# A pre-norm attention and feed-forward block on one core: the warming matmuls read a constant of ones, and some of them become 128 columns wide

## Chip, core and metric

The kernel runs on one core of one Trainium2 chip. The metric is device time in microseconds (us), the median of three executions. Five engines work side by side and meet at semaphores: TensorE (PE, with its weight loads shown apart as PEld), VectorE (DVE), ScalarE (ACT), GpSimd (POOL) and SyncE (SP), which issues nearly all of the transfers.

## What is computed

The input x has 2048 rows of 640 numbers in bf16. The block is a layer norm, a linear attention with 32 heads of 20 columns, a residual, a second layer norm, and a gated feed-forward layer of width 1536 with its residual:

```python
qkv = layernorm(x) @ wqkv                      # 640 -> 3 * 640
pq, pk = q @ w_phi[h], k @ w_phi[h]            # per head, 20 x 20
phi(p) = concat(softmax(p), softmax(-p))       # 40 features
kv, z = phi(pk).T @ v, sum(phi(pk))
o = (phi(pq) @ kv) / (phi(pq) @ z + 1e-6)
h = x + o @ wo
out = h + (gelu(layernorm(h) @ w_gate) * (layernorm(h) @ w_up)) @ w_down
```

The warming matmuls are no part of this. They multiply a constant by itself into a PSUM tile, `wu`, that nothing reads.

## The kernel before

The 2048 rows are 16 tiles of 128 rows, in four groups of four tiles. The order of work is written out by hand for all engines (the schedule is manual), so each engine runs its instructions in the order in which the code issues them.

The beginning is what matters for the change:

- Line 171 and on: SP issues the loads in one queue, one after another. First come tiles of x and pieces of the value weights `Wv`, then from line 188 five transposing loads of the key weights into `WkT` (line 186), one for each block of 128 input columns.
- Lines 194 to 197: DVE clears `zero`, a tile of 128 x 512, and then sets the ones columns of eight value tiles `vS`.
- Lines 207 to 212: TensorE runs nine warming matmuls of 512 columns, each with its own weight load, on `zero`.
- `ln_0` (line 246) computes the statistics of tile 0 and the centred tile `xc` (line 250). `tr_c(0)` transposes it on TensorE in five matmuls of 128 columns (line 147), and ACT copies the result to `LN1T` (line 148). `tr_c(1)` does this for tile 1, with the copy on DVE.
- `warm(WA)`, between the transposes of tile 0 and the first value matmuls, issues two more warming matmuls of 512 columns.
- `v_part` (line 290) multiplies the transposed tile by parts of `Wv`, as these arrive.
- `fold` (line 228) multiplies `WkT` by a block-diagonal matrix made of `w_phi`; five column blocks, the last of which needs the last of the five transposing loads. Copies on DVE (line 239) and ACT (line 237) bring the result to `Wk2`, which the key matmuls (line 274) need.

After that come a loop over the 16 tiles (keys, values and their products; the folded query weights; `load_T` of `WqT`), the query matmuls (line 362), the attention outputs, and the feed-forward layer (lines 615 and 636), which takes most of the time.

The tile `zero` lies in a pool `fp` that is closed before the loop. The framework that the kernel is written in has a preamble: POOL fills four one-column constants (line 749 in the profile, the place where the program is built), one of them 1.0 in bf16, and the engines then meet at a barrier before the body begins.

Of the kernel before, what the change touches and what calls it, by code (L numbers as in the profile page):

```python
# [8 lines left out]
BF16 = mybir.dt.bfloat16  # L9
# [8 lines left out]
def kernel(  # L18
# [12 lines left out]
    nc = tc.nc  # L31
    P = 128
# [11 lines left out]

    H0 = [(P * c) // Dh for c in range(NC)]
    NH = [(P * c + P - 1) // Dh - H0[c] + 1 for c in range(NC)]
    NWARM = 9
    VP = (0, 2, 4, 6, 9, 11)
    KA, QA = (1,3), (0,1,2,3,4)
    FQ = (4, 5, 6, 7, 8)  # L50

    QG = ((0, 1), (2, 3), (4, 5), (6,), (7, 8), (9, 10), (11, 12), (13, 14), (15,), (16,), (17,), (18,), (19,))
    QT = (15, 15, 15, 15)
    WA = 2
    T3 = 4

    KVG = {5: (0, 1), 9: (2, 3, 4, 5), 13: (6, 7, 8, 9), 15: (10, 11)}
# [42 lines left out]
    def gtile(name):  # L100
        return psG.tile([P, 2, 512], F32, name=name, tag="G")
# [62 lines left out]
    fp = fp_cm.__enter__()  # L164
# [26 lines left out]
    wu_v = B_w_up.rearrange("(c p) n -> p c n", p=P)  # L191


    zero = fp.tile([P, 512], BF16, name="zero")
    nc.vector.memset(zero, 0.0)
    for i in range(8):
        nc.vector.memset(vS[i][:, :, Dh], 1.0)
    make_identity(nc, ident)
# [6 lines left out]
                                compare_op=ALU.is_ge, fill=0.0, base=Dh - 1 - off, channel_multiplier=-1)  # L205

    wu = gtile("wu")
    def warm(n):
        for _ in range(n):
            nc.tensor.matmul(wu[:, 0, :], lhsT=zero[:, 0:P], rhs=zero, start=True, stop=True)  # L210

    warm(NWARM)

    def fold(WT, W2, halves, ds=range(NC)):

# [30 lines left out]
    def ln_0(t):  # L246
        xt, mean, rstd, _ = lnp[t] = ln_stats(p1, [x_sb[0][:, t, :]], f"c{t}", False, None, True)[0]
        nc.gpsimd.tensor_scalar(nrstd[t], rstd, -1.0, None, op0=ALU.mult)
        xc = fp.tile([P, D], BF16, name="xc", bufs=2)
        nc.vector.tensor_scalar(xc, xt, mean, None, op0=ALU.subtract)  # L250
        return xc

    def ln_st(*tiles, act=True, between=None, log=False):
        for t, v in zip(tiles, ln_stats(p1, [x_sb[t // 4][:, t % 4, :] for t in tiles], "1", act, between, log)):
            lnp[t] = v
# [138 lines left out]
    xc = [ln_0(t) for t in CT[:1]]  # L394
    tr_c(0)
    xc.append(ln_0(1))
    warm(WA)
    ln_st(2, act=False, log=True)
    v_part(0, 0, 1)
    tr_c(1)  # L400
# [364 lines left out]
```

## Time and profile before

| | |
|---|---|
| median of three executions | 279.65 us |
| the three executions | 279.73, 279.65, 278.71 us |
| profiled execution, first to last instruction (span) | 277.2 us |
| busy time of DVE, ACT, POOL | 167.3, 143.5, 94.7 us |
| warming matmuls | 11, the first at 1.24 us |
| first useful matmul (transpose of `xc`) | 4.73 us |
| DMA queues' share of 16 engines (first queue) | 30.8% |

The page gives no time of the profiled execution other than its span. The span is 2.45 us below the median and 1.5 us below the fastest of the three executions; start and end of an execution lie outside it.

How to read it: times in a timeline count from the first instruction of the span. A line of a timeline has the start, the length, the engine, the source line, the operation with what it writes and reads, and the count. In brackets stands the engine's idle time before it and what ended that idle time. A matmul's own time is its latency; several in a row overlap, so the distance from one start to the next is what one costs.

### The profile page before, as it was taken

Reading aid. Unit: us, or ns where it says so; the run is one execution under the profiler, and the core shown is the slowest. Engines: PE = TensorE matmul, PEld = TensorE weight load, DVE = VectorE, ACT = ScalarE, POOL = GpSimd, SP = SyncE. Lnnn points to the kernel's source line nnn. Section 1 sums busy time; section 2 is a strip of 40 time slices with the busy share of each in tenths; the row PEclk is TensorE's granted clock in tenths of the full one; section 3 lists DMA queues with packets and bytes.
Section 4 is the critical chain, followed back from the end, with each engine's and each line's share of the span. In section 5 each row is a group of like instructions: output and inputs, shape, how many; then the busy total and the mean of one; then the engine's idle time right before and its main releaser. Section 6 shows DMA issues by size and latency. Waiting matters only on the chain.

```text
span 277.2 us, 5817 instructions
## 1 busy us (share of the span) xinstructions
PE 271.6 (98%) x2337; PEld 172.1 (62%) x2337; DVE 167.3 (60%) x292; ACT 143.5 (52%) x239; POOL 94.7 (34%) x213
## 2 busy tenths in 40 slices
PE   7899999999999999999999999999999999999995
PEld 3677777764555887788754555675455567444574
DVE  6799999899496776675325757322666622233222
ACT  4879998778598755374524364413445440222200
POOL 4348997765202217365301353400226230000000
PEclk9999999999999999999999999999999999999999
DMA  7965732489730021324120213130022413000011
GB/s 204 192 232 112 99 74 47 44 256 393 255 102 0 4 47 36 85 49 77 30 65 2 47 27 63 32 88 33 14 36 25 73 25 95 26 0 0 0 50 47
DMA packets 42235, 21.37 MB, mean 77 GB/s; under 512 B 35040, under 2 KB 40416, under 8 KB 42208
## 3 DMA queue, kind: packets, MB, share of 16 engines
q1 hardware_dynamic: 42208, 21.01, 30.8%
q8 instruction: 18, 0.29, 0.5%
q14 instruction: 9, 0.07, 0.1%
HBM read 10.18 MB, written 2.62 MB: 46 GB/s over the span
## 4 chain that ended last, share of the span: by engine, by line
PE 87%; SPq 3%; DMA 3%; DVE 2%; ACT 2%; issue 1%
PE gu L615 38%; PE pd L636 19%; PE pq L362 8%; PE po L570 8%; PE pk L274 5%; PE pv L274 4%; PE ab L510 3%; PE kvp L340 2%; SPq L186 2%; DMA LN1T<-ln 2%; DVE stats L110 1%; DMA WkT<-in_A_wqkv_dram 1%; ACT E L307 1%; ACT ln L134 1%; PE wa L228 1%
## 5 line engine op out<-in xcount | busy, mean ns | idle before, releaser
L621 DVE TENSOR_TENSOR GT<-gu,g 128x512 bf16<-128x512 f32 (+1 forms) x60 | 34.4, 580 | 54.3 <-ACT g L618 54.1
L618 ACT ACTIVATE g<-gu 128x512 bf16<-128x512 f32 (+1 forms) x60 | 30.7, 512 | 69.3 <-PE gu L615 68.5
L615 PE MATMUL gu<-LN2T,Wg 128*128 128x512 bf16 (+1 forms) x300 | 61.9, 337 | 0.1
L615 PE MATMUL gu<-LN2T,Wu 128*128 128x512 bf16 (+1 forms) x300 | 61.8, 337 | 0.0
L636 PE MATMUL pd<-Wd,GT 128*128 128x320 bf16 (+2 forms) x396 | 53.8, 295 | 0.0
L636 PEld LDWEIGHTS <-GT 128*128 128x128 bf16 x396 | 37.9, 98 | 15.3 <-DVE GT L621 0.9
L615 PEld LDWEIGHTS <-Wu 128*128 128x128 bf16 x300 | 29.3, 98 | 22.6
L615 PEld LDWEIGHTS <-Wg 128*128 128x128 bf16 x300 | 28.3, 98 | 20.8
L274 PEld LDWEIGHTS <-LN1T 128*128 128x128 bf16 x290 | 27.9, 98 | 11.0 <-DMA LN1T<-ln 0.3
L322 POOL TENSOR_TENSOR vt<-vS,rs 128x672 bf16<-128x672 bf16 x22 | 29.1, 1344 | 9.1 <-DVE rs L318 7.4
L641 DVE TENSOR_TENSOR y<-pd,x_sb 128x640 bf16<-128x640 f32 (+3 forms) x18 | 13.5, 749 | 30.2 <-PE pd L636 30.2
L518 ACT COPY AB<-ab 128x704 f32<-128x704 f32 x28 | 19.6, 748 | 19.8 <-PE ab L510 19.6
L551 DVE TENSOR_TENSOR tt<-AB,w 128x1280 bf16<-128x1280 f32 x16 | 23.8, 1486 | 1.0 <-POOL w L544 0.9
L570 PE MATMUL po<-Wo,oT 128*128 128x320 bf16 x160 | 24.3, 299 | 0.0
L274 PE MATMUL pk<-Wk,LN1T 128*128 128x320 bf16 x160 | 24.0, 299 | 0.0
L314 DVE TENSOR_REDUCE sk<-E 128x64 f32<-128x1280 bf16 x16 | 22.9, 1434 | 1.2 <-ACT E L307 1.2
L362 PE MATMUL pq<-LN1T,Wq 128*128 128x512 bf16 x100 | 22.9, 379 | 0.0
L367 ACT ACTIVATE Eq<-pq 128x1024 bf16<-128x1024 f32 (+1 forms) x26 | 19.9, 830 | 2.4 <-PE pq L362 2.4
L307 ACT ACTIVATE E<-pk 128x640 bf16<-128x640 f32 x28 | 18.3, 716 | 4.5 <-PE pk L274 4.3
L570 PEld LDWEIGHTS <-oT 128*128 128x128 bf16 x160 | 15.6, 98 | 7.0 <-ACT oT L148 0.3
L274 PE MATMUL pv<-Wv,LN1T 128*128 128x320 bf16 x130 | 19.8, 299 | 0.2 <-DMA LN1T<-ln 0.2
L134 ACT ACTIVATE ln<-x_sb,v,rstd 128x640 bf16<-128x640 bf16 x14 | 12.9, 919 | 11.3 <-POOL v L598 11.1
(101 smaller groups left out, 268.1 us busy)
## 6 DMA issues: line engine op xcount, KB each, us to landing
out_dram<-y SPq DMA_DIRECT2D x15, 160.0 KB, 1.8
Wg<-in_B_w_gate_dram SPq DMA_DIRECT2D x1, 1920.0 KB, 9.4
Wu<-in_B_w_up_dram SPq DMA_DIRECT2D x1, 1920.0 KB, 15.3
Wd<-in_B_w_down_dram SPq DMA_DIRECT2D x1, 1920.0 KB, 7.9
x_sb<-in_A_x_dram SPq DMA_DIRECT2D x2, 640.0 KB, 5.5
Wo<-in_A_wo_dram SPq DMA_DIRECT2D x1, 800.0 KB, 11.1
x_sb<-in_A_x_dram SPq DMA_DIRECT2D x4, 160.0 KB, 3.1
Wv<-in_A_wqkv_dram SPq DMA_DIRECT2D x2, 320.0 KB, 4.1
```

Of the source, the lines that this page charges most:

```text
L274: nc.tensor.matmul(ps[:, u, 0:HD], lhsT=lnT(t, c), rhs=W[:, c, u * HD:(u + 1) * HD], start=(c == 0), stop=(c == NC - 1))
L307: nc.scalar.activation(Ek[t][:, s, :].rearrange("p (u f) -> p u f", u=2), pk[:, :, 0:HD], ACTF.Exp, scale=((lnp[t][2], nrstd[t]) if t in C ...
L314: nc.vector.reduce_sum(sk, Ek[t].rearrange("p s (h f) -> p (s h) f", f=Dh), axis=AX.X)
L322: eng.tensor_tensor(vt[:, s], vS[t % 8], rs[:, s * H:(s + 1) * H, None].to_broadcast([P, H, VC]), ALU.mult)
L362: nc.tensor.matmul(pqs[j][:, i, :], lhsT=Wq2[:, kc, c * P:(c + 1) * P], rhs=LN1T[b][:, kc, :], start=(kc == 0), stop=(kc == NC - 1))
L367: nc.scalar.activation(Eq[j][:, :, s, :], pqs[j][:, 0:len(QG[j])], ACTF.Exp, scale=(1.0, -1.0)[s])
L551: nc.vector.tensor_tensor(tt.rearrange("p s (h f) -> p s h f", f=Dh), num, w[:, :, :, None].to_broadcast([P, 2, H, Dh]), ALU.mult)
L570: nc.tensor.matmul(po[:, u, 0:HD], lhsT=st[t][:, c, :], rhs=Wo[:, c, u * HD:(u + 1) * HD], start=(c == 0), stop=(c == NC - 1))
L615: nc.tensor.matmul(gu[:, i, 0:n], lhsT=W[:, c, f * P:(f + 1) * P], rhs=LN2T[b][:, c, a0:a1], start=(c == 0), stop=(c == NC - 1))
L618: nc.scalar.activation(g[:, 0:n], gu[:, 0, 0:n], ACTF.Gelu_apprx_tanh)
L621: nc.vector.tensor_tensor(st[b, "g", f][:, a0:a1], gu[:, 1, 0:n], g[:, 0:n], ALU.mult)
L636: nc.tensor.matmul(pd[:, u, n0:n1], lhsT=st[b, "g", f][:, tl * P:(tl + 1) * P], rhs=Wd[:, f, u * HD + n0:u * HD + n1], start=(f == 0), sto ...
```

## The change

The tile `zero` and its clearing on DVE go. The warming matmuls read the preamble's constant of one bf16 column, seen as 128 x 512 by a column step of zero, for weights and for the moving operand alike. The function `warm` takes a list of widths. The nine matmuls of 512 columns at the start become seven of 512 and eight of 128 (4608 columns before and after); the two of 512 behind the transposes of tile 0 become seven of 128 (1024 columns before, 896 after). TensorE has 22 instructions more, DVE one fewer; the order of all others is the same on every engine.

```diff
-    NWARM = 9
...
-    WA = 2
...
-    zero = fp.tile([P, 512], BF16, name="zero")
-    nc.vector.memset(zero, 0.0)
+    ones = nc.const_aps.tensor(1.0, [P, 512], BF16)
     for i in range(8):
         nc.vector.memset(vS[i][:, :, Dh], 1.0)
...
     wu = gtile("wu")
-    def warm(n):
-        for _ in range(n):
-            nc.tensor.matmul(wu[:, 0, :], lhsT=zero[:, 0:P], rhs=zero, start=True, stop=True)
-
-    warm(NWARM)
+    def warm(*cols):
+        for n in cols:
+            nc.tensor.matmul(wu[:, 0, 0:n], lhsT=ones[:, 0:P], rhs=ones[:, 0:n], start=True, stop=True)
+
+    warm(*[512] * 7, *[P] * 8)
...
     xc = [ln_0(t) for t in CT[:1]]
     tr_c(0)
     xc.append(ln_0(1))
-    warm(WA)
+    warm(*[P] * 7)
     ln_st(2, act=False, log=True)
     v_part(0, 0, 1)
     tr_c(1)
```

## The prediction

> **What bounds the kernel now.** I read the page's busy times first, then the chain that ended last, then the timeline of TensorE over the first 16 us, where the change lies. The page says that the kernel as a whole is bound by TensorE:
>
> ```profile
> PE 271.6 (98%) x2337; PEld 172.1 (62%) x2337; DVE 167.3 (60%) x292; ACT 143.5 (52%) x239; POOL 94.7 (34%) x213
> ```
>
> 98% is an average, and the warming matmuls count as busy in it. What a change in the first 5 us is worth is read from the chain through the first 16 us. There, TensorE is not on it:
>
> ```profile
> 0.73 0.07 issue
> 0.79 0.40 SPq L171
> ...
> 5.20 1.30 SPq L186
> ...
> 9.18 1.28 SPq L186
> 10.46 0.04 issue
> 10.50 3.23 DMA WkT<-in_A_wqkv_dram
> 13.73 0.04 issue
> 13.77 0.51 PE wa L228 x6
> 14.28 0.02 issue
> 14.30 0.04 DVE Wk L239
> ```
>
> The columns are start, length and what it was. The reader is to see that from 0.79 to 10.5 us the chain is SP issuing one load after another: nine plain ones of 0.40 to 0.52 us and five transposing ones of about 1.28 us. It then waits 3.2 us for the last transposing load to land, and only at 13.77 us does it reach TensorE, with the fold that needs this load. No warming matmul, no transpose of `xc` and no value matmul is in it. After 14.3 us it goes on through DVE and ACT, whose busy shares from 16 to 28 us are nearly whole (DVE 3.90 of 4.00 and 7.93 of 8.00 us), and at 32.9 us it comes to TensorE to stay.
>
> The second view is the timeline of the first 6 us, TensorE's matmuls first, and then the last of its weight loads:
>
> ```profile
> 1.24 3.55 PE L210 MATMUL wu<-zero 128*128 128x512 bf16 x9 [1.24 <-DVE zero L195]
> 4.73 0.45 PE L147 MATMUL tp<-ident,xc 128*128 128x128 bf16 x5
> 5.02 0.59 PE L210 MATMUL wu<-zero 128*128 128x512 bf16 x2
> 5.96 0.72 PE L290 MATMUL pv<-Wv,LN1T 128*128 128x320 bf16 x4 [0.35 <-ACT LN1T L148]
> ```
>
> ```profile
> 3.35 0.15 PEld L210 LDWEIGHTS <-zero 128*128 128x128 bf16 x1 [0.27 <-issue]
> 3.78 0.15 PEld L210 LDWEIGHTS <-zero 128*128 128x128 bf16 x1 [0.28 <-issue]
> 4.20 0.10 PEld L210 LDWEIGHTS <-zero 128*128 128x128 bf16 x1 [0.27 <-issue]
> 4.72 0.28 PEld L147 LDWEIGHTS <-xc 128*128 128x128 bf16 x5 [0.43 <-DVE xc L250]
> ```
>
> Three things are to be seen. First, up to 4.20 us a warming matmul comes every 0.425 us, where a row of 10 matmuls of 512 columns in the feed-forward part takes 2.16 to 2.18 us on the chain, 0.217 each: TensorE runs at half its clock here, and the load at 4.20 us is the first short one (0.10 instead of 0.15 us). The granted clock in the profile reads 1.00 in these stretches too, so only the spacing shows the half clock. The clock rises about 2.95 us after the first warming matmul. Second, the transposes of tile 0 begin at 4.72 us since `xc` is done at 4.67 (it starts at 4.28 and takes 0.39), not since the warming matmuls end. Third, the value matmuls at 5.96 us wait for ACT's copy of the transposed tile (5.22 + 0.69 = 5.91), again not for the warming matmuls before them.
>
> **The change, part by part.**
>
> *The clearing of `zero` goes from DVE.* It is one instruction of 0.27 us at 0.91. DVE next sets eight columns of `vS` until about 2.3 us (1.25 + 1.08), and then idles 0.79 us until the first tile of x lands, at 3.12. So everything that DVE does for the chain starts when it does now: 0.
>
> *TensorE starts earlier.* Its first weight load waits for `zero` now (idle 1.24 us, released by DVE). The trace does not show when it would start without that wait. The earliest is 0.79 us, when SP, ACT and POOL leave the barrier; the latest is 1.24, as now. I take 0.91, where DVE, which waits at the same barrier, has its first instruction. That is 0.33 us earlier (bounds 0 and 0.45).
>
> *The first group has as many columns as before, 4608.* At 0.425 us per 512 columns this is 3.83 us, if the clock stays at half throughout. From 0.91 it ends at 4.74, against 5.07 now. If the clock rises at 4.18 us as in this execution, 3.27 us run at half clock (about 3940 columns), and the remaining 670 take 0.28 us at 0.217 per 512: the end is at 4.46. The eight narrow ones also need a weight load each. The five transposes show what that is at full clock: they last 0.45 us in all, 0.22 of it the latency of one, so (0.45 - 0.22) / 4 = 0.058 us each, against 0.054 for 128 columns at 0.217 per 512. That is nothing to speak of. In this execution, then, the group ends 0.2 us ahead of `xc`, and the transposes begin at 4.72 as before: 0.
>
> *The second group* is 7 x 0.058 = 0.41 us instead of 2 x 0.217 = 0.43, and ends near 5.45 us. The copy that the value matmuls wait for ends at 5.91: 0. Its cover is 0.46 us; at half clock the group would be 7 x 0.107 = 0.75 instead of 0.85.
>
> *The narrow width* matters where a useful matmul comes ready while a warming one runs. It then waits at most 0.107 us at half clock instead of 0.425. In this execution nothing waits so: 0. In one whose clock rises only after 4.7 us, the ninth wide matmul would end at 5.07 and hold the transposes back 0.35 us; with the change they would start at about 4.74. That is the place where the change can gain.
>
> *The reuse of memory and PSUM.* Without `zero` the pool is 1 KB per partition smaller, and a few waits of TensorE on its own and ACT's earlier work in PSUM differ: one is added at the transposes of the third tile, two of its own kind and two on ACT go. The added one asks for work of TensorE from some 2 us earlier, so it finds it done. I cost it at 0; at worst it drains one 320-column matmul, 0.299 - 0.136 = 0.16 us, and TensorE idles 0.79 us between 6 and 14 us, which covers it. The other four can only take waiting away, in the loop; the same 0.16 each bounds them, and DVE and ACT are late there: 0.
>
> **Weighing a rule.** The trace has the clock at half for the 2.95 us that follow the first matmul. [...]
>
> **The sum** on the profiled execution is 0: span 277.2 us stays. The time before, 279.65, is a median of executions that lie 1.0 us apart, with the profiled span 1.5 us below the fastest. If part of that spread is the moment at which the clock rises, an execution gains between 0 and the 0.33 us of the earlier start. I take the middle, 0.15: 279.5 us.
>
> **Rivals.**
>
> *Most executions have a late clock, and the path then goes through TensorE.* For it: two of three executions are 1.0 us above the third, and TensorE idles only 0.35 us before the first value matmuls and 0.79 us from there to 13.77, so that a clock at half to 7.6 us would use the slack up (work of about 1.5 us doubled, less 1.14, is +0.4). Against it: in the one trace the chain runs through SP. The gain would be the 0.33 us of the start, 0.16 us of half clock saved by an equally earlier rise, together 0.5, and at most the 1.0 us of the spread: 279.15, down to 278.7.
>
> *Slower: the constant read at column step zero streams slower than a dense tile.* No row before shows TensorE reading with step zero. It decides from the point at which the first group ends later than 4.72 plus the slack of 1.14, that is at 5.86 us: (5.86 - 0.91) / 4608 columns is 1.07 ns a column against 0.83 now, 30% slower. At twice the time the group would end at 0.91 + 7.66 = 8.57 us, the transposes would be 3.85 us late, less 1.14 of slack: +2.7, 282.3 us. The lower bound is the rate of now, 0.425 us per 512 columns, and I take it, as the nearest row is the same matmul at the same widths. [...]
>
> [...] A rise at 7.6 us instead of 4.2 costs the +0.4 worked out above: 280.05.
>
> *The change doesn't do what it says*: TensorE starts no earlier than 1.24 us, because something else holds it. Then everything is as now: 279.65. This falls together with the forecast.
>
> **Chances.** Forecast, hidden, 0.66 (its own range 278.7 to 280.0, from the spread of the three executions and the 0.33); late clock and a gain 0.18; clock later 0.10; slow reads 0.06. The range takes in the late clock's gain to a little below 278.7, since the median of three can fall on the fast executions, and the later clock above 280.05 by the same spread: 278.3 to 280.5. About 0.5%, 1.4 us, is what a measurement of this kernel can tell from no change. Faster by that (under 278.25) needs the late clock in nearly all executions and the full spread: 0.11. Slower by that (above 281.05) is the slow reads and a part of the later clock: 0.08. The rest, 0.81, is within.
>
> **What would show it.** In the profile after: the first warming matmul near 0.9 us with no wait on DVE; wide ones still 0.425 us apart before the rise of the clock and narrow ones at most 0.11; `xc`'s transposes still at about 4.7 us, released by DVE; value matmuls at about 5.96, released by ACT; and the last load of `WkT` landing at 13.7 with the fold waiting for it. I am wrong if the fold at 13.77 us or the key matmuls after it move by more than 0.3 us, if the wide warming matmuls are more than 0.5 us apart, or if the short weight loads begin later than 4.7 us.

## The result, and the profile after

The kernel after takes 281.24 us (median of six executions, 280.58 to 281.59), the kernel before 279.67 us (median of six, 278.71 to 279.91). The ratio is 1.0065, 95% interval 1.0044 to 1.0085: the medians lie 1.57 us apart and the means 1.79, on the slower side. Forecast were 279.5 us, in a range from 278.3 to 280.5. The profiled execution after took 281.43 us, and its span is 279.7 us, 2.5 more than before.

The first view is the timeline of TensorE over the first 6 us of the kernel after, in the columns used before:

```profile
0.83 4.00 PE L207 MATMUL wu<-const-bfloat16-1.0 128*128 128x512 bf16 x15 [0.83 <-PEq L746]
4.73 0.55 PE L145 MATMUL tp<-ident,xc 128*128 128x128 bf16 x5
5.12 0.57 PE L207 MATMUL wu<-const-bfloat16-1.0 128*128 128x128 bf16 x7
6.06 0.72 PE L287 MATMUL pv<-Wv,LN1T 128*128 128x320 bf16 x4 [0.38 <-ACT LN1T L146]
```

The warming starts at 0.83 instead of 1.24 us and no longer waits for DVE. The transposes start at 4.73, where they started before, and the value matmuls at 6.06 instead of 5.96, since in this execution the clock rose during the transposes (0.55 us instead of 0.45; the trace's record of the clock begins with full clock at 4.96 us, in the trace before at 4.18). That is 0.1 us, and TensorE has idle time behind it (0.16 us before the value matmuls at 7.22, 0.51 before the transposes at 13.05). The loss is not here.

The second view is the chain through the first 30 us of the kernel after (start, length, what):

```profile
10.88 3.43 DMA WkT<-in_A_wqkv_dram
14.31 0.05 issue
14.36 0.50 PE wa L225 x6
...
27.70 0.80 ACT ln L132
28.50 0.61 ACT vS L291
29.11 0.04 issue
29.15 1.52 PE pk L271 x10
```

As before, the fold waits for the last transposing load; it landed 0.58 us later (14.31 instead of 13.73). What is new stands at 29.15 us: key matmuls that wait for ACT's copy of values. Before, nothing of that kind was on the chain there. The timeline of that place, TensorE and ACT of the kernel after:

```profile
26.20 1.52 PE L271 MATMUL pv<-Wv,LN1T 128*128 128x320 bf16 x10
28.39 0.70 ACT L291 ACTIVATE vS<-pv 128x640 bf16<-128x640 f32 x1
29.15 1.52 PE L271 MATMUL pk<-Wk,LN1T 128*128 128x320 bf16 x10 [1.43 <-ACT vS L291]
```

and TensorE at the same place of the kernel before:

```profile
25.61 1.52 PE L274 MATMUL pv<-Wv,LN1T 128*128 128x320 bf16 x10
26.97 1.52 PE L274 MATMUL pk<-Wk,LN1T 128*128 128x320 bf16 x10
28.33 0.48 PE L228 MATMUL wa<-BD,WqT 128*128 128x140 bf16 x6
```

Before, the key matmuls of tile 4 follow the value matmuls of tile 7 without a gap (1.36 us from start to start, ten times 0.136). After, TensorE stands still for 1.43 us, until ACT has copied those very values. From start to start it is 2.95 us, 1.59 more than before. There, the row that follows without a gap starts 0.16 us before the last matmul of the row ahead of it has ended (25.61 + 1.52 - 26.97), and that overlap is lost too. This place is 24 us behind the last warming matmul, and no line of the diff touches it.

**What the diff does there.** The matmuls of this kernel write to tiles in PSUM (`wu`, `tp`, `pv`, `pk`, `wa`, `kvp` in its lines), a memory that the kernel uses in slots, each a pair of banks, a tile of 128 x 2 x 512 in f32; a pool is a set of slots from which tiles take theirs in turn. At tile 4 (`T3`) the kernel closes a PSUM pool of four slots of two banks and opens one of three (`psG`) and one of one (`psK`, for `kvp`). The first key matmuls of tile 4 take the first pair of banks, and must wait for the last reader of whatever had these banks in the old pool. A pool hands a new tile the slot that the framework reckons free first. In the built programs, before, the fifth tile of the first pool (`pv` of tile 1) takes the banks of `wu`, and the sixth (`tp` of tile 2) those of the first transposed tile. After, it is the other way round, and these two slots stay swapped to the end of that pool. So the first pair of banks holds at its end the keys of tile 2 before, long read, but after the values of tile 7, the newest tile of all. In the program the same matmul waits for ACT's 33rd signal instead of its 27th.

The two profiled executions differ by 0.59 us at the fold (13.77 and 14.36), by 2.17 us at ACT's first exponential of tile 4 (28.53 and 30.70), and by 2.5 us at the end. The two lines of ACT, before and after:

```profile
28.53 1.30 ACT L307 ACTIVATE E<-pk 128x640 bf16<-128x640 f32 x2
30.70 1.30 ACT L304 ACTIVATE E<-pk 128x640 bf16<-128x640 f32 x2 [1.61 <-PE pk L271]
```

Between fold and exponential lie 1.58 us, the size of the loss in the medians.

### The profile page after: what moved, and what is told of

Same layout as the page of the kernel before. It is cut to its first block, busy times and chain, and to the rows that moved or that the text cites. A ratio compares the mean times of both kernels' runs of the same rounds, so it can differ in the third digit from the quotient of the medians.

```text
span 279.7 us, 5822 instructions
## 1 busy us (share of the span) xinstructions
PE 271.6 (97%) x2333; PEld 173.3 (62%) x2348; DVE 166.4 (59%) x291; ACT 143.4 (51%) x239; POOL 95.2 (34%) x213
## 4 chain that ended last, share of the span: by engine, by line
PE 86%; SPq 3%; ACT 3%; DMA 3%; DVE 2%; issue 1%; ACTq 0%
PE gu L612 37%; PE pd L633 19%; PE pq L359 8%; PE po L567 8%; PE pk L271 5%; PE pv L271 3%; PE ab L507 3%; PE kvp L337 2%; SPq L184 2%; DMA LN1T<-ln 2%; DVE stats L108 1%; ACT E L304 1%; DMA WkT<-in_A_wqkv_dram 1%; ACT ln L132 1%; ACT vS L291 1%
## 6 DMA issues: line engine op xcount, KB each, us to landing
Wo<-in_A_wo_dram SPq DMA_DIRECT2D x1, 800.0 KB, 10.5
```

## The experiments

Theory A: the loss is the order in which PSUM is handed out. Theory B: the warming matmuls themselves cost it (B1 the constant, B2 the narrow width). Each kernel is compared with the kernel before on the same chip; before had medians of 279.34 us (for experiments 1, 2, 3 and 6) and 279.08 us (for 4, 5, 7 and 8).

**1. Five narrow ones in the second group.**

```diff
-    warm(*[P] * 7)
+    warm(*[P] * 5)
```

> The kernel after, with five instead of seven narrow warming matmuls in the second group; all else of the change stays. Built so, PSUM is handed out in the order of the kernel before (the fifth tile takes the pair of banks of wu, not that of the first transpose). Theory A, bank order: the key matmuls of tile 4 no longer wait 1.4 us for ACT's copy of the values of tile 7, and the time falls back by about 1.6 us to the kernel before, ratio 0.997 to 1.002. Theory B, the constant or the narrow width itself costs (later clock, slower stream): the time stays near 281.2 us, ratio 1.005 to 1.008.

Measured: 279.8 us, ratio 1.0008 (0.9994 to 1.0023). Its TensorE at the change of pools:

```profile
26.62 1.52 PE L271 MATMUL pv<-Wv,LN1T 128*128 128x320 bf16 x10
27.98 1.52 PE L271 MATMUL pk<-Wk,LN1T 128*128 128x320 bf16 x10
```

The 1.36 us from start to start are back, and the loss is gone, with the constant, the early start and both narrow groups in place. Two narrow matmuls fewer are 0.12 us of work (five take 0.45 us, seven 0.57) that ends before 5.7 us; they can't be worth 1.5 us by their own length.

**2. The kernel before with four wide ones in the second group.**

```diff
-    WA = 2
+    WA = 4
```

> The kernel before, with four instead of two wide warming matmuls in the second group, still on the cleared tile. Built so, PSUM is handed out in the order of the kernel after. Theory A, bank order: the 1.4 us wait at the key matmuls of tile 4 appears although nothing of the change is in this kernel, and the time is 281.0 to 281.5 us, ratio 1.005 to 1.008. Theory B, the constant or the narrow width: the two more matmuls end by 5.9 us, before the value matmuls need TensorE, and the time is that of before, ratio 0.998 to 1.002.

Measured: 281.28 us, ratio 1.0066 (1.0048 to 1.0083): the loss of the change, with none of the change in it. Its line at the place:

```profile
29.57 1.52 PE L274 MATMUL pk<-Wk,LN1T 128*128 128x320 bf16 x10 [1.43 <-ACT vS L294]
```

The wait is 1.43 us, the same as after. Theory A fits, and B can't explain this one.

**3. The kernel before with the constant alone.**

```diff
-    zero = fp.tile([P, 512], BF16, name="zero")
-    nc.vector.memset(zero, 0.0)
+    zero = nc.const_aps.tensor(1.0, [P, 512], BF16)
```

> The kernel before, whose warming matmuls read the constant, at the old widths (nine and two of 512). Built so, PSUM is handed out in the order of the kernel after. Theory A, bank order: ratio 1.005 to 1.008, with the wait of 1.4 us at the key matmuls of tile 4. Theory B1, the constant costs: the same ratio, but with the loss in the first 6 us. Theory B2, the narrow width costs: ratio 0.998 to 1.002.

Measured: 280.88 us, ratio 1.0055 (1.0035 to 1.0074), with the same wait for ACT's copy of the values:

```profile
29.15 1.52 PE L273 MATMUL pk<-Wk,LN1T 128*128 128x320 bf16 x10 [1.43 <-ACT vS L293]
```

B2 can't explain this loss, as no narrow matmul is in the kernel. The time doesn't part A from B1, but the place does: the wait is at the change of pools. And experiment 1 has the constant without the loss.

**4. The kernel before with the narrow width alone**, on the cleared tile, in the second group.

```diff
-            nc.tensor.matmul(wu[:, 0, :], lhsT=zero[:, 0:P], rhs=zero, start=True, stop=True)
+            nc.tensor.matmul(wu[:, 0, 0:n], lhsT=zero[:, 0:P], rhs=zero[:, 0:n], start=True, stop=True)
...
-    warm(WA)
+    warm(*[P] * 7)
```

> The kernel before, on the cleared tile, with the second group of seven narrow instead of two wide warming matmuls, the nine wide ones unchanged. The banks are handed out in the order of before. Theory A: no loss, ratio 0.998 to 1.002. Theory B2, the narrow width itself costs: 1.005 to 1.008.

Measured: 279.48 us, ratio 1.0005 (0.9989 to 1.0021). The key matmuls of tile 4 start at 26.98 us, 1.36 behind the value matmuls at 25.62. The narrow width in the second group costs nothing that can be told from noise.

**5. All warming matmuls of the change, the second group into a tile of its own.**

```diff
+    wu = gtile("wu")
     warm(*[P] * 7)
```

> The kernel after with every warming matmul of the change, but the second group writes to a PSUM tile of its own instead of wu. Built so, the key matmuls of tile 4 get banks whose last reader is ACT's second exponential of tile 3, and kvp keeps the banks that it has before and after. Theory A, the loss is only the order of the banks where the PSUM pools change: the wait of 1.4 us shrinks to 0 to 0.25 us and the last pool change is as before; ratio 0.999 to 1.003. Theory B, something in the warming matmuls themselves costs time that five instead of seven hid: ratio 1.005 to 1.008.

Measured: 280.04 us, ratio 1.0024 (1.0010 to 1.0038). TensorE at the change of pools:

```profile
26.09 1.52 PE L271 MATMUL pv<-Wv,LN1T 128*128 128x320 bf16 x10
27.64 1.52 PE L271 MATMUL pk<-Wk,LN1T 128*128 128x320 bf16 x10
```

1.55 us from start to start instead of 1.36: of the delay of 1.59 us, 0.19 is left; in the built program the banks now depend on ACT's second exponential of tile 3. With every matmul of the change kept, most of the loss is gone. About 0.7 us of 279.08 remain by the ratio, of which 0.19 is explained; the rest is not settled.

**6. The kernel after, with the two pools opened in the other order.**

```diff
-            psG = ps_cm.enter_context(tc.tile_pool(name="psG", bufs=3, space=PSUM, reuse_waits="tile"))
             psK = ps_cm.enter_context(tc.tile_pool(name="psK", bufs=1, space=PSUM, reuse_waits="tile"))
+            psG = ps_cm.enter_context(tc.tile_pool(name="psG", bufs=3, space=PSUM, reuse_waits="tile"))
```

> The kernel after, with all of its warming matmuls; only the two PSUM pools of the loop from tile 4 on are opened in the other order, so that the accumulator kvp takes the banks that ACT frees last and the key matmuls of tile 4 take banks that ACT frees at about 27.7 us, when TensorE comes there. Theory A, bank order: the wait of 1.4 us goes or shrinks to under 0.2, and the time is 279.3 to 280.0 us, ratio 0.998 to 1.001. Theory B: unchanged by this, ratio 1.005 to 1.008.

Measured: 281.51 us, ratio 1.0075 (1.0055 to 1.0095). The expectation missed. The first wait did go: the key matmuls start 1.55 us behind the value matmuls, as in experiment 5. But its TensorE later shows this:

```profile
70.82 1.24 PE L337 MATMUL kvp<-vt,E 128*64 128x84 bf16 x56
73.52 2.32 PE L359 MATMUL pq<-LN1T,Wq 128*128 128x512 bf16 x10 [1.47 <-DVE KV L349]
```

`kvp` now lies in the first pair of banks, and at the next change of pools the first query matmuls need it. They wait 1.47 us for DVE's masked copy out of `kvp`. In experiment 1 the query matmuls start at 72.05 us without a wait. One handover was mended and the other broken, at the same price.

**7. The same exchange of pools in the kernel before.**

> The kernel before, with the two PSUM pools of the loop opened in the other order, no change in the warming. kvp then holds the first pair of banks, which the first query matmuls behind the last pool change need. Theory A says that a wait at a change of pools costs its own length wherever TensorE is the bound: TensorE idles some 1.5 us there until the masked copy of kvp is done, and at the first change at most 0.3 us: 280.8 to 281.4 us, ratio 1.005 to 1.007. If only the first change of pools mattered, ratio 0.999 to 1.001.

Measured: 281.18 us, ratio 1.0071 (1.0050 to 1.0093), and the wait is at the last change of pools:

```profile
73.63 2.32 PE L362 MATMUL pq<-LN1T,Wq 128*128 128x512 bf16 x9 [1.48 <-DVE KV L352]
```

So such a wait can be made without touching the warming at all, and it costs about its own length, here with a gap of 0.19 us at the first change (28.40 after 26.85, less 1.36).

**8. Hardly any warming:** one narrow matmul in each group, the banks in the order of before.

```diff
-    warm(*[512] * 7, *[P] * 8)
+    warm(P)
...
-    warm(*[P] * 7)
+    warm(P)
```

> The kernel after with one narrow warming matmul in each group instead of 15 and 7; the banks are handed out in the order of before. If the warming is worth something, the clock rises about 3 us later than the 4.2 to 5.8 us seen so far, the transposes and value matmuls of the first tiles run at half clock, and up to 1.5 us of TensorE work is doubled, less 1.1 us of idle time: +0.4 to +1 us, ratio 1.001 to 1.004. If the first 14 us are bound by the loads alone, 0.999 to 1.001.

Measured: 281.16 us, ratio 1.0068 (1.0044 to 1.0092), more than expected. TensorE in the first 14 us:

```profile
4.67 0.71 PE L145 MATMUL tp<-ident,xc 128*128 128x128 bf16 x5 [3.58 <-DVE xc L247]
5.18 0.31 PE L207 MATMUL wu<-const-bfloat16-1.0 128*128 128x128 bf16 x1
6.46 1.22 PE L287 MATMUL pv<-Wv,LN1T 128*128 128x320 bf16 x4 [0.96 <-DMA Wv<-in_A_wqkv_dram]
7.48 0.74 PE L145 MATMUL tp<-ident,xc 128*128 128x128 bf16 x5
8.04 3.10 PE L287 MATMUL pv<-Wv,LN1T 128*128 128x320 bf16 x12
10.98 0.44 PE L145 MATMUL tp<-ident,ln 128*128 128x128 bf16 x5
```

Twelve value matmuls take 3.10 us, nearly all at half clock, instead of 1.79, and only the transposes at 10.98 have the 0.44 us of full clock. The chain of this kernel runs through TensorE from 6.46 us on, not through SP and `WkT`. By the ratio this kernel is 1.9 us slower than before (0.0068 x 279.08), and only with the warming are the first 14 us bound by the loads. Against the profiled execution before, ACT is 1.2 us late at 34.5 us, behind a chain that runs through these slow rows; another 1.1 us come between 203 and 229 us, with two waits (0.54 and 0.18 us) for transposed attention outputs. Whether these belong to the warming is not settled.

No version tried beats the kernel before beyond its interval; the nearest are experiments 1 and 4, equal to it.

## Why the prediction was wrong, point by point

- *The clearing of `zero`, the earlier start, the columns of the first group, the second group, the narrow width: 0 each.* Right, as far as the runs can tell. The first group started 0.41 us earlier (0.33 was taken), a wide warming matmul on the constant takes the same 0.425 us (weight loads at 2.06, 2.49, 2.92 us), and the transposes started at 4.73. Experiment 1 has all of these, with two narrow ones fewer, and a ratio of 1.0008; its interval leaves room for at most 0.6 us.
- *The reuse of memory and PSUM: 0.* This is the step that failed. The prediction saw that four waits of TensorE in the loop had gone, and wrote that they "can only take waiting away". They had gone because one earlier wait had grown to cover them: the key matmuls of tile 4, which waited for ACT before and after, wait six signals later after. The prediction went by which engine a wait names, and not by the count behind it. It bounded the price by draining one matmul, 0.16 us; the runs show an idle time of 1.43 us, 1.59 from start to start. The remark that DVE and ACT are late there spoke for a price: the later signal of the late ACT was a stall of 1.43 us.
- *Weighing a rule.* The moment at which the clock rises does vary: 2.95 us after the first warming matmul before, 4.13 after, and later in experiment 3, where the transposes at 4.76 us, 3.93 after that matmul, still take 0.72 us instead of 0.45. What it depends on, no run shows. Nor does a run show the 0.15 us that the sum takes as a gain from it: experiment 1, which starts as early, is no faster than before.
- *Most executions have a late clock, and that makes the 1.0 us between executions*: not borne out. In the four profiled executions without a wait of over 0.2 us at a change of pools, the warming in place, that spread goes with the landing of the fourth tile of x (four cases, no test of its own; the two short ones are kernels on the cleared tile, the two long ones on the constant). ACT's square of that tile starts at 8.27 and 8.48 us in the two with spans of 277.2 and 277.0, and at 9.03 and 9.35 in those with 278.3 and 278.4. Late landings are not the constant's alone: on the cleared tile, that square starts at 9.47 and 9.65 us in experiments 2 and 7. But all six traces on the constant have it late (8.92 to 9.35), so a small cost of the earlier start by way of the loads is not excluded, within the 0.6 us of experiment 1. Why the tile lands later in some is open.
- *Slower by reads at column step zero*: excluded by the 0.425 us and by experiment 1. The time fell above 281.05, to which the prediction gave 0.08, but that chance rested on this rival and on the later clock, and neither names the mechanism.
- *The clock rises later*: it did, at 4.96 instead of 4.18 us in the two profiled executions, and cost 0.1 us at the value matmuls. The rise at 7.6 us, from which the prediction had its 0.4 us, is shown by no run: before, after and in experiments 1 to 5 the first value matmuls, at 5.96 to 6.26 us, run about 0.14 us apart, at full clock (four take 0.72 us), and in experiment 8, with hardly any warming, four take 1.22 us at 6.46, and the rise comes at about 10.7.
- *The signs of being wrong.* Three of them came: the fold moved by 0.59 us, the short weight loads began later than 4.7 us, with the clock, and the key matmuls of tile 4 moved by 2.18 us (26.97 and 29.15). Only the last of these holds the loss: in experiment 1, as fast as before, the profiled fold is at 14.79 us, 1.02 later.
- *A reading of the chain.* Up to 10.5 us the chain before holds four transposing loads, not five. SP issues the fifth from 10.50 to 11.78 us, so the last piece of 3.23 us is 1.28 of issue and about 1.95 until it has landed. The sum doesn't rest on it.

## What to carry to other kernels

Where pools pick their slots by a reckoning of what is free first, a small change to early, harmless work can permute the slots, and the price falls due at the next change of pools, far from the diff. So compare in the built programs which banks each tile gets and the counts behind the waits, not only the order of the instructions; a wait that disappears may have been swallowed by a larger one. When a handover is mended, follow the moved tile to its next handover: the accumulator in experiment 6 gave the same loss back 45 us later.

## What the hardware showed

- With hardly any warming, experiment 8 was 1.9 us of 279.08 slower: the clock rose only at about 10.7 us, 6 us after the first transposes (an estimate from the twelve value matmuls between 8.04 and the transposes at 10.98 us, 0.136 us apart at full clock and twice that at half). TensorE had been idle for 3.58 us before these and for 0.96 us before the first value matmuls; whether such gaps or the missing matmuls delayed the clock is not shown.
- Seven narrow matmuls with a weight load each took 0.55 us from first start to last end at full clock in experiment 4, (0.55 - 0.22) / 6 = 0.055 us apart, with 0.22 us the latency of one transpose. By the column that is on par with the 512-column matmuls of the feed-forward part at full clock, 0.217 us each, or 0.054 for 128 columns.
- Why the framework's reckoning puts the two slots in one order for two or three wide or five narrow matmuls, and in the other for four wide, seven narrow on the constant, or two wide on the constant, was not studied; the built programs show only that it does.
